# Half of the first product's column groups as two Strassen units, pooling moved into the second product, batch 2 pooled as rows

## The chip, the cores and the metric

The kernel runs on one core of one Trainium2 chip. The metric is the device time in microseconds (us) of the slowest core, here the only one. Profile pages are of one execution. "Fast" and "slow" are the two states of a run: slow is a run more than 1.5% above the fastest of the same kernel, and verdicts use fast runs only. "Faster" and "slower" ask for a ratio clear of 2%; within that is "same". Engines are called PE (the matrix engine), DVE (vector), ACT (scalar), POOL and SP; the last two issue transfers here.

## The reference, cut to what matters

```python
# q, k, v: (8 batches, 8 heads, 576, 64); w_in: (512, 2048); w_out: (2048, 512)
k_p = k.reshape(B, H, 72, 8, D).mean(axis=3)        # keys and values pooled by 8
v_p = v.reshape(B, H, 72, 8, D).mean(axis=3)
attn = softmax(q @ k_p^T / 8)
x = (attn @ v_p) -> (4608 tokens, 512)
h = x @ w_in                                         # first product, "up"
out = silu(h) @ w_out                                # second product, "down"
```

## The kernel before

Tokens go through in nine tiles of 512. Tile t has an up (16 groups of 128 columns of `w_in`, four matmuls of 512 columns each) and a down. From tile 1 on, the down is one Strassen level: seven products of quarters in place of eight, with sums of weights made once (`weight_sum`) and sums of the hidden values made in each tile (`hidden_sum`). Beside tile t's down PE computes the attention of batch t+1, which gives `xT` for the next tile. One core's engines work through their own queues in program order, and the program places small work ("fillers") between matmuls by step numbers.

```python
def spread(fillers, n):                 # a filler at step i is put behind step i
    todo = sorted(fillers, key=lambda f: f[0])
    for i in range(n):
        yield i
        while todo and todo[0][0] <= i:
            todo.pop(0)[1]()
...
def select_v(b, a, tag="at"):           # pooled rows -> heads, by selection matmuls
    if a == 0:
        st["v_ps"] = ps_tile([128, H, D], FP32, tag, "v_ps")     # one bank for both halves
    ... nc.tensor.matmul(st["v_ps"][:SP, h, :], lhsT=shifts[...], rhs=v5[:n, i], ...)
def copy_v(b, a, copy=nc.vector.tensor_copy):
    copy(out=vp[:, heads of half a], in_=v_ps[:SP, heads of half a])
...
def numerators(b, g, f):                # 8 matmuls, then two multiplies on DVE:
    nc.vector.tensor_mul(out=xT[:, 2 * g + c, cols], in0=nu[c][:, :HS], in1=rec)
...
# down_quarters: product order and the first sums on DVE
KA = KQ - 2
product(2, 0, KA); product(5, 0, KA); product(2, KA, KQ)
nc.vector.tensor_copy(out=r_sb, in_=ps["P"])
product(5, KA, KQ)
tt(out=rr_sb, in0=ps["Q"], in1=r_sb, op=add)
...
# schedule of tile t, a = t + 1 (cut)
items = [(g, 0, NTT) for g in range(KG)]                  # 16 plain groups
f_up.append((0, lambda: pool_k(a)))                       # pooling beside the up
f_up.append((10, lambda: pool_v(a)))
f_up.append((1, lambda: load_one(a + 1, "k")))            # first half of the next keys (SP)
f_up.append((2, lambda: load_rest(a + 1, "k")))           # second half, added by the transfer (POOL)
f_down: scores at steps 1, 28, 56, 77; denominators 28, 46, 69, 89; numerators 46, 69, 89, 93
```

The softmax here doesn't subtract the row's maximum and nothing guards it: scores larger than these inputs give would overflow.

## Time and profile before

| | before |
|---|---|
| time, median of the runs beside the changed kernel | 295.86 us (295.78 to 296.62) |
| span in the profile | 294.7 us |
| PE busy / idle | 287.9 / 6.8 us |
| DVE, ACT busy | 65%, 60% |
| start of tile 1; tiles 1 to 8 (us each) | 54.2; 31.7 30.6 30.1 30.5 30.3 30.8 26.0 30.5 |

A tile's length is read from PE's timeline, from its first matmul to that of the next tile. Two more rows of the page matter: the busy tenths of PE in 40 equal slices of the span, and the clock that PE was granted in them.

```profile
PE   8999999999999999999999999999999999999995
...
PEclk9999999999999999999999999999999999999998
```

In every slice between the first and the last PE is busy for 90% or more, and its granted clock is 90% or more. In the lines below, names in `_ps` are buffers in PSUM that matmuls write: `hp_ps` and `u_ps` for the up, `o_ps` for the down, `sc_ps`, `den_ps` and `nu_ps` for scores, denominators and numerators, `kz_ps` and `v_ps` for selected keys and values; `xT` is the input of the up, `h_T` the hidden values, `es` the exponentials.

### The profile page before, as it was taken

How to read it: one execution, taken by the hardware profiler on the slowest of the kernel's cores; microseconds unless marked ns; L12 is line 12 of the kernel's file. 1: busy time of each engine (PE TensorE's matmuls, PEld its weight loads, DVE VectorE, ACT ScalarE, POOL GpSimd, SP SyncE). 2: the span in 40 equal slices, each digit the busy share in tenths (PEclk: the TensorE clock that was granted, in tenths of full speed). 3: DMA queues.
4: the chain of work that ended last, by engine and by line, in shares of the span. 5: the costliest groups of instructions: out<-in, count | busy, mean ns of one | idle time of the engine just before them, and what ended most of it. 6: DMA issues, size and time to landing. Idle time of an engine off the chain costs nothing.

```text
span 294.7 us, 6052 instructions
## 1 busy us (share of the span) xinstructions
PE 287.9 (98%) x2417; PEld 175.6 (60%) x2417; DVE 191.2 (65%) x344; ACT 177.6 (60%) x366; POOL 42.8 (15%) x60
## 2 busy tenths in 40 slices
PE   8999999999999999999999999999999999999995
PEld 3348434446564666457788774476547654884584
DVE  4886445999978566865586659666865642741562
ACT  1677675567566865676667675776577666407500
POOL 8654100001300120013001710110000000000000
PEclk9999999999999999999999999999999999999998
DMA  7999999958794797487857895783500032004003
GB/s 215 271 282 205 247 229 180 209 147 174 106 177 108 160 132 136 106 177 111 150 128 162 120 122 137 167 116 51 123 20 2 2 89 53 2 22 117 6 12 135
DMA packets 34909, 37.65 MB, mean 128 GB/s; under 512 B 9856, under 2 KB 26368, under 8 KB 34880
## 3 DMA queue, kind: packets, MB, share of 16 engines
q0 software_dynamic: 20128, 18.50, 37.3%
q1 hardware_dynamic: 14176, 17.84, 26.5%
q10 hardware_dynamic: 576, 0.92, 0.9%
q8 instruction: 19, 0.31, 0.5%
q14 instruction: 10, 0.08, 0.1%
HBM read 36.70 MB, written 9.44 MB: 157 GB/s over the span
## 4 chain that ended last, share of the span: by engine, by line
PE 86%; DVE 10%; ACT 1%; issue 1%; DVEq 0%
PE hp_ps L428 37%; PE o_psQ L535 14%; PE o_psP L535 14%; PE o_psR L535 4%; PE sc_ps L348 4%; PE o_ps L462 4%; PE warm_ps L583 4%; PE nu_ps L388 3%; DVE raw L197 3%; DVE h_sum L495 2%; PE den_ps L365 2%; DVE w_sum L513 2%; DVE qT L148 1%; DVE xT L396 1%; PE kz_ps L313 1%
## 5 line engine op out<-in xcount | busy, mean ns | idle before, releaser
L428 PE MATMUL hp_ps<-xT,w_in_sb 128*128 128x512 bf16 (+3 forms) x684 | 128.2, 345 | 0.4 <-ACT h_T L434 0.4
L434 ACT ACTIVATE h_T<-hp_ps 128x512 bf16<-128x512 f32 (+2 forms) x155 | 87.4, 567 | 57.4 <-PE hp_ps L428 45.3
L428 PEld LDWEIGHTS <-w_in_sb 128*128 128x128 bf16 x684 | 65.9, 98 | 56.6 <-issue 1.5
L495 DVE TENSOR_TENSOR h_sum<-h_T 128x1024 bf16<-128x1024 bf16 (+2 forms) x88 | 52.0, 637 | 36.1 <-ACT h_T L434 36.1
L535 PEld LDWEIGHTS <-h_sum 128*128 128x128 bf16 x640 | 60.9, 98 | 15.1 <-issue 6.5
L356 ACT ACTIVATE es<-sc_ps 72x288 bf16<-72x288 f32 x128 | 41.4, 403 | 13.2 <-PE sc_ps L348 13.1
L396 DVE TENSOR_TENSOR xT<-nu_ps,rec 128x288 bf16<-128x288 f32 x64 | 25.7, 448 | 12.0 <-PE nu_ps L388 11.8
L535 PEld LDWEIGHTS <-h_T 128*128 128x128 bf16 x256 | 23.6, 98 | 6.5 <-issue 4.1
L177 POOL DMA_DIRECT2D raw<-in_k_dram x5 | 7.1, 1420 | 114.5 <-DVE h_sum L495 48.4
L148 DVE STREAM_TRANSPOSE qT<-q_bf 128x576 bf16<-128x576 bf16 x32 | 23.6, 758 | 0.0
L374 ACT ACTIVATE lnd<-den_ps 128x288 f32<-128x288 f32 x30 | 12.3, 411 | 16.6 <-PE nu_ps L388 9.8
L197 DVE TENSOR_TENSOR raw<-raw 72x1024 f32<-72x1024 f32 (+1 forms) x18 | 19.7, 1094 | 0.1
L291 DVE TENSOR_TENSOR raw<-raw 128x768 f32<-128x768 f32 (+3 forms) x16 | 10.5, 654 | 11.1 <-DMA raw<-in_v_dram 7.8
L535 PE MATMUL o_psP<-w_out_sb,h_sum 128*128 128x256 bf16 x128 | 17.6, 273 | 0.0
L535 PE MATMUL o_psQ<-w_out_sb,h_sum 128*128 128x256 bf16 x128 | 17.6, 273 | 0.0
L535 PE MATMUL o_psQ<-w_sum,h_T 128*128 128x256 bf16 x128 | 17.5, 274 | 0.0
L535 PE MATMUL o_psP<-w_sum,h_sum 128*128 128x256 bf16 x128 | 17.0, 273 | 0.5 <-DVE o_sb L556 0.5
L535 PE MATMUL o_psP<-w_sum,h_T 128*128 128x256 bf16 x128 | 16.5, 273 | 0.0
L535 PE MATMUL o_psR<-w_sum,h_sum 128*128 128x256 bf16 x128 | 16.5, 273 | 0.0
L462 PE MATMUL o_ps<-w_out_sb,h_T 128*128 128x512 bf16 x64 | 15.9, 381 | 0.0
L535 PE MATMUL o_psQ<-w_sum,h_sum 128*128 128x256 bf16 x128 | 15.4, 273 | 0.0
L348 PE MATMUL sc_ps<-qT,kz 32*72 32x288 bf16 x256 | 14.4, 295 | 0.9 <-DVE xT L396 0.7
(58 smaller groups left out, 212.0 us busy)
## 6 DMA issues: line engine op xcount, KB each, us to landing
out_dram<-o_sb SPq DMA_DIRECT2D x128, 64.0 KB, 1.7
raw<-in_k_dram SPq DMA_DIRECT2D x8, 512.0 KB, 5.2
raw<-in_v_dram SPq DMA_DIRECT2D x7, 512.0 KB, 6.9
q_bf<-in_q_dram POOLq DMA_DIRECT2D x6, 576.0 KB, 11.8
raw<-in_k_dram POOLq DMA_DIRECT2D x5, 576.0 KB, 9.1
raw<-in_v_dram POOLq DMA_DIRECT2D x5, 576.0 KB, 9.9
w_in_sb<-in_moe_w_in_dram POOLq DMA_DIRECT2D x8, 256.0 KB, 8.5
w_out_sb<-in_moe_w_out_dram POOLq DMA_DIRECT2D x4, 512.0 KB, 13.7
```

The costliest lines, as they stand in the source:

```text
L148: nc.vector.transpose(out=st["qT"][:, a, f * QF : (f + 1) * QF].rearrange("r i c p -> r (i c p)"), in_=st["q_bf"][:, a, f * n : (f + 1) * n],)
L197: nc.vector.tensor_add(out=raw[:, :, :w], in0=raw[:, :, :w], in1=raw[:, :, w : 2 * w])
L348: nc.tensor.matmul(sc[s], lhsT=kz[b % 2][rows, g, c, :], rhs=st["qT"][rows, g, f * QF : (f + 1) * QF, c, :], start=(c == 0), stop=(c == 1),)
L356: nc.scalar.activation(es[:, s, :], sc[s], func=AF.Exp, scale=score_scale)
L374: nc.scalar.activation(lnd, den_ps[:, :HS], func=AF.Ln)
L396: nc.vector.tensor_mul(out=xT[:, 2 * g + c, cols], in0=nu[c][:, :HS], in1=rec)
L428: nc.tensor.matmul(hp_ps[:, r0:r1], lhsT=w_in_sb[:, kk, g * 128 : (g + 1) * 128], rhs=xT[:, kk, x0 : x0 + r1 - r0], start=(kk == 0), stop= ...
L434: nc.scalar.activation(h_T[:, g, n0 : n0 + n], hp_ps[:, :n], func=AF.Silu)
L462: nc.tensor.matmul(ps, lhsT=h_T[:, g, m * 128 : (m + 1) * 128], rhs=w_out_sb[:, g, :], start=(g == 0), stop=(g == KG - 1),)
L495: nc.vector.tensor_tensor(out=h_sum[n][:, ks, :], in0=quarter(*a, ks), in1=quarter(*b, ks), op=op)
L535: nc.tensor.matmul(ps[b][:, c, :], lhsT=left(n, kt, c), rhs=W_OUT[n][:, kt, :], start=b not in begun, stop=kt == KQ - 1, skip_group_check= ...
L583: nc.tensor.matmul(warm_ps, lhsT=warm[:, :128], rhs=warm, start=True, stop=True)
```

## The change

The intent is fewer matmuls. Column groups 4 to 7 and 8 to 11 of the up become Strassen "units" (the first of them only in tile 1, both in tiles 2 to 8): seven products of four matmuls of 256 columns, 28 in place of 16 of 512. Sums of `w_in` are made once in tile 0, five sums of `xT` in every tile, four sums from PSUM per unit, all on DVE. To make room, pooling of the keys goes into the down of the tile before, pooling of the values and two of four q transposes go into the down of the same tile, and two copies go to ACT. Batch 2, which was loaded as heads, is loaded as pooled rows and selected by matmuls; that frees buffer space. Products 2 and 5 of the down now begin with their second halves (KA is KQ // 2), whose column groups are ready first. Cut to its core:

```diff
+    def stage(y, n):                       # unit y, product n
+        if n == "2": product(y, 2, "P", True);  nc.scalar.copy(r_sb, ps["P"])
+        elif n == "5": product(y, 5, "Q", True);  tt(out=rr_sb, in0=ps["Q"], in1=r_sb, op=ALU.add)
+        elif n == "1": product(y, 1, "R", True);  tt(out=t_sb, in0=ps["R"], in1=rr_sb, op=ALU.subtract)
+        elif n == "4": product(y, 4, "P", False); hidden(y, 1, 0, ps["P"])      # Silu
+        elif n == "3": product(y, 3, "Q", False); hidden(y, 0, 1, ps["Q"])
+        elif n == "7": product(y, 7, "P", False); tt(out=c_sb[0], in0=ps["P"], in1=t_sb, op=ALU.add)
+        ...
...
-            items = [(g, 0, NTT) for g in range(KG)]
+                items = (G(12, 13) + [(0, "251")] + G(14) + [(0, "43")] + G(15) + [(0, "76")]
+                    + [(1, "2")] + [(0, "s")] + [(1, "51")] + G(0) + [(1, "43")] + G(1)
+                    + [(1, "76")] + G(2) + [(1, "s")] + G(3))
+            for n in U_X:
+                f_up.append((0, lambda n=n: unit_x_sum(t, n)))
+            for n in (2, 5, 1, 6):
+                f_up.append((46 if t == 1 else 36, lambda n=n: hidden_sum(n, 4, 8)))
+            for n in (2, 5, 1):
+                f_up.append((64, lambda n=n: hidden_sum(n, 0, 4)))
+            f_down.append((60, lambda: hidden_sum(6, 0, 4)))
...
+            elif t == 1:                    # batch 2 as rows
+                    f_down.append((8 + 10 * j, lambda j=j: slot_sums("v", j)))
+                    f_down.append((40 + j, lambda j=j: select_v(2, j, "at")))
+                    f_down.append((40 + j, lambda j=j: copy_v(2, j)))
             else:
-                f_up.append((0, lambda: pool_k(a)))
+                f_down.append((10, lambda: pool_v(a)))
...
+                for y in range(2):          # tile 0
+                    for n in U_W:
+                        f_up.append((22 + 14 * y, lambda y=y, n=n: unit_weight_sum(y, n)))
+                    f_down.append((43 + 7 * j, lambda j=j: slot_sums("k", j)))
             elif a + 1 < B:
+                f_down.append((50, lambda: pool_k(a + 1, 0)))
+                f_down.append((81, lambda: pool_k(a + 1, 1)))
                 f_up.append((1, lambda: load_one(a + 1, "k")))     # kept where it was
                 f_up.append((2, lambda: load_rest(a + 1, "k")))
```

## The prediction

> **What bounds the kernel now.** I read the page's busy shares first, then the chain that ended last in order of time, then the timelines of VectorE (DVE) and ScalarE (ACT) around the places where that chain leaves TensorE (PE). The page and the per-core view give clock 0.997 and:
>
> ```profile
> PE 287.9 (98%) x2417; PEld 175.6 (60%) x2417; DVE 191.2 (65%) x344; ACT 177.6 (60%) x366; POOL 42.8 (15%) x60
> ```
>
> PE is idle for only 6.8 us of 294.7. The kernel has nine token tiles (t = 0 to 8), each with a first product ("up") and a second ("down"). The chain prices both:
>
> ```profile
> 238.30 13.81 PE hp_ps L428 x64
> ...
> 257.35 1.75 PE o_psP L535 x16
> ```
>
> A plain up of 64 matmuls of 512 columns takes 13.81 us, 0.2158 each; 16 matmuls of 256 columns take 1.75 us, 0.109 each, although each has its own weight load of 98 ns: the load hides. The windows by tile give 30.1 to 30.8 us for tiles 2 to 6, 26.0 for tile 7 (no attention beside it), 30.4 for tile 8 with its tail. So work removed from PE is worth its full time, as long as nobody makes PE wait.
>
> The 65% of DVE hides one place where DVE is already the bound. From 50.3 to 77.4 us the chain runs on DVE; its timeline is gapless at the end of tile 0:
>
> ```profile
> 48.35 0.82 DVE L396 TENSOR_TENSOR xT<-nu_ps,rec 128x288 bf16<-128x288 f32 x2 [0.45 <-PE nu_ps L388]
> 49.35 0.69 DVE L470 COPY o_sb<-o_ps 128x512 f32<-128x512 f32 x1 [0.18 <-PE o_ps L462]
> 49.95 0.81 DVE L396 TENSOR_TENSOR xT<-nu_ps,rec 128x288 bf16<-128x288 f32 x2
> 50.68 1.42 DVE L513 TENSOR_TENSOR w_sum<-w_out_sb 128x512 bf16<-128x512 bf16 x4
> 52.02 0.81 DVE L396 TENSOR_TENSOR xT<-nu_ps,rec 128x288 bf16<-128x288 f32 x2
> 52.75 1.42 DVE L513 TENSOR_TENSOR w_sum<-w_out_sb 128x512 bf16<-128x512 bf16 x4
> 54.09 0.81 DVE L396 TENSOR_TENSOR xT<-nu_ps,rec 128x288 bf16<-128x288 f32 x2
> ```
>
> The last pair writes the xT that tile 1's first group reads in its third and fourth matmul; PE starts that group at 54.37, so it comes some 0.3 us early, no more. The end of that DVE chain is the only real wait of PE in mid-kernel:
>
> ```profile
> 77.39 0.40 PE L348 MATMUL sc_ps<-qT,kz 32*72 32x288 bf16 x5 [0.67 <-DVE xT L396]
> ```
>
> Three of eight score matmuls ran, the fourth wanted a PSUM buffer that DVE had yet to empty: five buffers rotate, and the third scores of a tile reuse the first numerators' buffer.
>
> A steady tile has slack instead. Tile 3 (up ends, "T0", at 130.5):
>
> ```profile
> 131.18 1.28 ACT L401 ACT_TABLE_LOAD   x1
> 132.47 1.30 ACT L356 ACTIVATE es<-sc_ps 72x288 bf16<-72x288 f32 x4
> ```
> ```profile
> 131.19 1.36 DVE L495 TENSOR_TENSOR h_sum<-h_T 128x512 bf16<-128x512 bf16 x3 [0.89 <-ACT h_T L434]
> 134.10 0.69 DVE L548 COPY r_sb<-o_psP 128x512 f32<-128x512 f32 x1 [1.54 <-PE o_psP L535]
> 134.71 1.22 DVE L495 TENSOR_TENSOR h_sum<-h_T 128x2048 bf16<-128x2048 bf16 x1
> 135.84 0.68 DVE L550 TENSOR_TENSOR rr_sb<-o_psQ,r_sb 128x512 f32<-128x512 f32 x1
> 137.34 0.82 DVE L396 TENSOR_TENSOR xT<-nu_ps,rec 128x288 bf16<-128x288 f32 x2 [0.82 <-PE nu_ps L388]
> ```
>
> Before the first numerators are emptied DVE idles 1.54 + 0.82 us, and the third scores come at 138.5, another 0.8 after the first buffer is free. The exponentials end at 133.77 and the denominators want them at 134.1.
>
> **What the Trainium skill says.** "TensorE: Matmul & The Clock Gate", Wait — 56ns, not 53.3ns?: start to start is N/2.4 + about 2.5 ns warm, 109 ns for N = 256; the trace agrees (1.75/16). "VectorE: DVE Perf Modes", The perf-mode tier table: tensor_tensor is 2x in bf16 from SBUF and 1x with a PSUM operand; the trace has 0.355 us a step for 512 bf16 elements (1.42 for four) and 0.61 (0.69 alone) for 512 with a PSUM operand. "PSUM — Partial Sum Buffer", Engine vs sequencer instructions: the queues of VectorE and ScalarE are strict FIFO; the timelines agree, each keeps the program's order, so a sum placed ahead of a numerator delays it in full.
>
> **The change, part by part.**
>
> *PE.* A unit replaces four groups, 16 x 0.2158 = 3.45 us, by 28 matmuls of 256 columns, 28 x 0.109 = 3.06: 0.39 saved. One unit in tile 1, two in tiles 2 to 8: 15 units, -5.9 us. Batch 2 as rows brings 24 + 12 selection matmuls (12 moved PE by 0.2 to 0.3 us in tile 0, 6 by 0.2 to 0.3) less four transposes (0.13): about +0.8. Net -5.1 us: this alone would give 290.7.
>
> *DVE, steady tile.* Added: five x sums (5 x 0.355 = 1.8) and four PSUM sums a unit (8 x 0.61 = 4.9). Removed: key copy 0.3 and one output copy 0.61, both to ACT. Net +5.8 on 20 to 21 us a tile, some 26.5 of 29.5: near 90%. Moved from up into down: pooling, two q transposes, one hidden sum: 4.65 + 1.4 + 0.6 us. The down side goes from about 9.6 to 15.7 us against 16.2 of PE.
>
> *DVE, tile 0.* Ten w_in sums (3.55 us) go ahead of batch 1's key row sums; batch 2's key row sums (1.86 + 1.43) and the first piece of w_sum 4 (0.36) go ahead of the last numerators. Tile 1 loses two head trees of pooling (each two trees of about 2.3 us) and gets value row sums (3.3), copies (1.4), its unit and x sums (4.3) and pooling for batch 3 (2.0): no lighter.
>
> Now the places in order.
>
> (a) Tile 0, key selection: the row sums end at 25.4 and 26.9, PE wants them at 28.2 and 29.3; pushed by 3.55 they end at 29.0 and 30.4. PE waits about 1.1 us.
>
> (b) Start of tile 1: 1.86 + 1.43 + 0.36 = 3.65 us more in a gapless DVE queue with 0.3 of slack: 3.3 us of PE wait.
>
> (c) First numerators of tile 1: they need the values' copy, which stands behind the last w_sum pieces 1.1, x sums 1.8, unit 2.5, copies 0.6, transposes 1.4, w_sum 7 and half of 6 2.1, hidden sums 2.4 + 1.8, transpose 0.7, value row sums 3.3, r_sb 0.6, hidden sum 7 1.1, transpose 0.7, rr 0.6, copy 0.4: 21 us from the end of (b), plus about 2 in which DVE waits for PE. PE gets there 2.9 us sooner; before lost 0.67 nearby: +2.2.
>
> (d) Tiles 2 to 6. In up, unit 1's last PSUM sums stand behind four hidden sums (4 x 0.6), which wait for t_sb, about 9.4 us into the up: DVE reaches them at 11.8 instead of 11.0, and the ACT queue ends its last Silu about 1.65 us after T0 instead of 0.7. Table load and exponentials then end at T0 + 4.2, where the denominators want them at 3.7: half a microsecond of wait. From that last Silu DVE has, before the first numerators are emptied: hidden sums 1.8, transpose 0.7, value pooling 1.85, r_sb 0.61, hidden sum 7 1.13, transpose 0.7, rr 0.61, first multiply 0.37 = 7.8: T0 + 9.4, against scores at T0 + 8.0. Both waits together: 1.35 us in tiles 2 and 3. Tiles 4 to 6 empty four numerators there, and scores need the third: T0 + 10.2 against 8.2, 1.9 us. Sum 2 x 1.35 + 3 x 1.9 = 8.4. Were ACT not late at all (0.7), it would still be 2 x 0.3 + 3 x 0.8 = 3.0. I take the middle, 5.7.
>
> (e) Tiles 7 and 8: the second part of product 2 comes 1.75 us after T0, its hidden sum at 2.3: 0.5; tile 8 hides most of it in the 0.52 us that its product 7 waited before: 0.15.
>
> Sum: -5.1 + 1.1 + 3.3 + 2.2 + 5.7 + 0.6 = +7.8: 303.6 us. I say 303.5.
>
> **The rivals.**
>
> *The gain arrives.* PE is 98% busy, DVE and ACT are at 65 and 60%, so the added sums fill idle time and 290 to 292 remain. For it: the shares, and a matmul schedule that leaves 1 to 2 us for every sum inside the units. Against it: the idle time of DVE is in up and at fixed points, the additions in (b) and (d) stand in a FIFO ahead of what PE wants next. For (b) I see no way round.
>
> *DVE becomes the bound throughout.* Then the tile lasts 26.5 us of DVE work plus its waits for PE and ACT, some 3.6 us (1.8 in the units, 1.65 at T0): about 30.1 to 31.5, and with (a) to (c) 305 to 308.
>
> *Transfers.* Batch 2's keys arrive on POOL's queue behind w_out, which landed at 43.4; 1.2 MB behind it at the 0.29 MB/us of that stretch is there by 47.5, before DVE asks at 49. Pooling for the next batch is now asked for about 23.5 us into a tile, while its second half is issued about 15 us in and takes 9.1 (page, issues): it could cost up to 1 us a tile, 3 in all: 306.
>
> **Range and chances.** The low end has (d) at 3.0, (c) at 1 and (a) hidden: 298.6; with a unit chain looser than I drew it, 297.5. The high end has (d) at 8.4 and late keys: 308. The 2% line is at 301.8. (b) plus the low (d) already eats the 5.1 us, so faster by over 2% is very unlikely; whether it stays under 301.8 hangs on (c) and (d).
>
> **What would show it.** Matmul cost: units at 0.109 us a matmul and up of tiles 7 and 8 near 13.0 us. (a): PE idle at about 28 us with DVE's key row sums as releaser. (b): 3 us of PE wait on xT at the start of tile 1. (c): numerators of tile 1 waiting for the vp copy. (d): in tiles 2 to 6 denominators waiting for es and the third scores waiting for xT, 1 to 2 us a tile, DVE near 90%. I am wrong if PE stays 98% busy and tiles 2 to 6 last 29.6 us; then the time is 291 to 293. If only (b) and (c) show, it is about 298.

## More of the kernel before

The stores of a tile's results stand in SP's queue at the end of its down, ahead of the loads of the next keys.

The waits of PE between 15 and 100 us (what waited, for whom, us in all, how often, the longest) are three, and small:

```profile
PE sc_ps L348 <- DVE xT L396: 0.7, 1, 0.7
PE hp_ps L428 <- ACT h_T L434: 0.4, 1, 0.4
PE sc_ps L348 <- DVE qT L148: 0.3, 1, 0.3
```

## The result, and the profile after

| | before | after |
|---|---|---|
| median of four fast runs | 295.86 us | 318.80 us (316.40 to 319.72) |
| span in the profile | 294.7 | 314.6 |
| start of tile 1 | 54.2 | 56.5 |
| tiles 1 to 8 | 31.7 30.6 30.1 30.5 30.3 30.8 26.0 30.5 | 39.6 31.3 31.6 35.6 31.6 32.0 26.1 30.4 |

The ratio is 1.0764, with a 95% interval of 1.0708 to 1.0821: slower. A ratio here is the mean time of one kernel's fast runs over that of the other's in the same rounds, so not quite the ratio of the medians; a fifth fast run (319.56 us) counts in it. The profile is of the fastest of the runs, 316.4 us; the others have no trace. In the two traces 19.9 us were added, and the tiles place them: tiles 0 and 1 together +10.2 (before ended them at 85.9, after at 96.1), tiles 2 to 6 +9.8, of which tile 4 alone +5.1, tiles 7 and 8 together -0.1.

The page of the changed kernel, its busy shares and the same two rows:

```profile
PE 293.3 (93%) x2597; PEld 192.3 (61%) x2597; DVE 235.2 (75%) x429; ACT 184.4 (59%) x393; POOL 46.2 (15%) x62
...
PE   8998999699599999999899969999999999999985
...
PEclk9999999999899999999999997999999999999999
```

PE is idle for 21.3 us now. More than that: it is busy for 5.4 us longer although less was asked of it, and in or just behind two of the three gaps of PE's row (the 5 and the second 6) the clock row shows a drop. The page's chain that ended last accounts for only some 5% of this span and can't be used; the list of PE's waits from 15 us on can:

```profile
PE sc_ps L323 <- DVE xT L371: 4.6, 7, 2.1
PE v_ps L306 <- DVE vp L313: 3.9, 1, 3.9
PE hp_ps L510 <- DVE xT L371: 2.8, 2, 1.5
PE o_psP L615 <- DVE h_sum L575: 2.5, 7, 0.7
PE kz_ps L288 <- DVE kz L295: 0.9, 2, 0.5
PE kz_ps L288 <- DVE k L270: 0.6, 1, 0.6
```

The third line, and of the last two the 0.61 and 0.45 us that fall in tile 0 (the keys of batch 1), are about as the prediction drew them. The rest comes in the places below.

**Start of tile 1.** DVE's timeline at the end of tile 0 has the new key row sums (L266) and the piece of `w_sum` ahead of the last numerators:

```profile
49.73 1.54 DVE L266 TENSOR_TENSOR raw<-raw 128x768 f32<-128x768 f32 x2
...
53.91 1.14 DVE L266 TENSOR_TENSOR raw<-raw 128x512 f32<-128x512 f32 x2
...
58.04 0.81 DVE L371 TENSOR_TENSOR xT<-nu_ps,rec 128x288 bf16<-128x288 f32 x2
```

The last pair starts at 58.04, 3.95 us later than it did (54.09). PE waits twice here, 1.45 us for the last pair but one and 1.33 us for the last (the first two lines of the next view).

**The values of batch 2, in tile 1's down.** PE's timeline:

```profile
56.47 0.74 PE L510 MATMUL hp_ps<-xT,w_in_sb 128*128 128x512 bf16 x2 [1.45 <-DVE xT L371]
58.54 3.33 PE L510 MATMUL hp_ps<-xT,w_in_sb 128*128 128x512 bf16 x14 [1.33 <-DVE xT L371]
...
79.01 0.27 PE L615 MATMUL o_psR<-w_sum,h_sum 128*128 128x256 bf16 x1
83.14 0.48 PE L306 MATMUL v_ps<-v,shifts 128*72 128x64 bf16 x6 [3.86 <-DVE vp L313]
```

The first half of the values was selected at 78.81; the second half goes into the same PSUM tile, whose first copy DVE reached only at 82.69. What came then is in the windows view (start and end, us; busy time of PE, PEld, DVE, ACT, POOL with counts; granted clock; share and rate of transfers), cut where the granted clock changes:

```profile
79.28:83.14 3.86, 0.00 (x1) 0.00 (x0) 3.78 (x7) 0.11 (x1) 0.00 (x0) 1.00 0.63 153
...
83.66:87.07 3.41, 3.41 (x24) 1.49 (x24) 2.03 (x5) 0.86 (x2) 2.17 (x2) 0.50 0.02 2
87.07:90.48 3.41, 3.41 (x43) 2.32 (x42) 2.72 (x6) 2.32 (x7) 0.00 (x0) 1.00 0.90 123
```

PE went on at 83.14, still at full clock; from 83.66 to 87.07 it was granted half, and then all of it again. That stretch lost 3.41 x 0.50 = 1.7 us, on top of the 3.86 of the wait, and the wait list doesn't show it.

**Keys of the next batch, tile 4.** Key pooling now stands at step 50 of the down, ahead of numerators. In tile 4 the keys were not there. SP's queue in that stretch (start, us, transfers issued):

```profile
158.12 11.83 SPq L530 DMA_DIRECT2D out_dram<-o_sb  x16
170.05 1.17 SPq L172 DMA_DIRECT2D raw<-in_k_dram  x2
```

POOL's timeline, with the second half's issue:

```profile
176.17 1.41 POOL L181 DMA_DIRECT2D raw<-in_k_dram  x1 [18.29 <-DVE h_sum L575]
```

DVE's timeline, where it pools the keys:

```profile
186.05 1.22 DVE L187 TENSOR_TENSOR raw<-raw 72x1024 f32<-72x1024 f32 x1 [2.59 <-DMA raw<-in_k_dram]
```

And PE's:

```profile
188.30 0.40 PE L323 MATMUL sc_ps<-qT,kz 32*72 32x288 bf16 x5 [2.12 <-DVE xT L371]
```

The tile began at 158.95. SP was busy issuing the 16 stores of the tile before and came to the keys' first half 11 us into the tile; POOL issued the second half, which is added onto the first, at 17; it was usable at 27. DVE waited 2.59 us, the numerators behind it came late, PE waited 2.12 us for a PSUM buffer, and its clock dropped again:

```profile
186.06:189.47 3.41, 1.29 (x16) 0.88 (x13) 2.96 (x5) 0.82 (x3) 1.13 (x2) 1.00 0.08 16
189.47:192.89 3.42, 3.42 (x26) 1.86 (x25) 1.78 (x6) 2.22 (x5) 3.42 (x7) 0.50 0.65 78
192.89:196.30 3.41, 3.41 (x25) 2.30 (x24) 2.27 (x5) 1.00 (x2) 1.52 (x3) 1.00 1.49 149
```

That is 3.42 x 0.50 = 1.7 us once more.

**Every tile from 2 to 6, behind T0 (the end of the up).** Tile 2, T0 at 109.4, DVE's timeline:

```profile
111.09 1.89 DVE L575 TENSOR_TENSOR h_sum<-h_T 128x1024 bf16<-128x1024 bf16 x3 [1.59 <-ACT h_T L516]
112.91 0.77 DVE L152 STREAM_TRANSPOSE qT<-q_bf 128x576 bf16<-128x576 bf16 x1
113.60 1.18 DVE L187 TENSOR_TENSOR raw<-raw 72x1024 f32<-72x1024 f32 x1
114.82 0.69 DVE L192 TENSOR_TENSOR vp<-raw 72x512 bf16<-72x512 f32 x1
115.43 0.68 DVE L628 COPY r_sb<-o_psP 128x512 f32<-128x512 f32 x1
116.03 1.21 DVE L575 TENSOR_TENSOR h_sum<-h_T 128x2048 bf16<-128x2048 bf16 x1
...
118.43 0.80 DVE L371 TENSOR_TENSOR xT<-nu_ps,rec 128x288 bf16<-128x288 f32 x2
```

After 1.59 us of idling for ACT's last Silu there is no gap until the first numerators are emptied at T0 + 9.0. PE pays at three points: it waits 0.22 us for the hidden sum, its four denominator matmuls take 0.64 us where later ones of the same tile take 0.31 (they wait for the exponentials inside the group), and it waits 0.54 us for the scores' buffer.

```profile
111.84 1.05 PE L615 MATMUL o_psP<-w_out_sb,h_sum 128*128 128x256 bf16 x8 [0.22 <-DVE h_sum L575]
...
113.37 0.64 PE L340 MATMUL den_ps<-es,ones 72*32 72x288 bf16 x4
...
118.92 0.40 PE L323 MATMUL sc_ps<-qT,kz 32*72 32x288 bf16 x5 [0.54 <-DVE xT L371]
```

### The profile page after: what moved, and what is told of

It reads as the page before. It is cut to its first block, busy times and chain, and to the rows that moved or that the text cites. A ratio compares the mean times of both kernels' runs of the same rounds, so it can differ in the third digit from the quotient of the medians.

```text
span 314.6 us, 6608 instructions
## 1 busy us (share of the span) xinstructions
PE 293.3 (93%) x2597; PEld 192.3 (61%) x2597; DVE 235.2 (75%) x429; ACT 184.4 (59%) x393; POOL 46.2 (15%) x62
## 5 line engine op out<-in xcount | busy, mean ns | idle before, releaser
L510 PE MATMUL hp_ps<-xT,w_in_sb 128*128 128x512 bf16 (+3 forms) x412 | 82.7, 340 | 3.2 <-DVE xT L371 2.8
L516 ACT ACTIVATE h_T<-hp_ps 128x512 bf16<-128x512 f32 (+2 forms) x95 | 51.6, 546 | 38.3 <-PE hp_ps L510 37.5
L575 DVE TENSOR_TENSOR h_sum<-h_T 128x1024 bf16<-128x1024 bf16 (+1 forms) x72 | 50.2, 743 | 12.9 <-ACT h_T L516 11.8
L510 PEld LDWEIGHTS <-w_in_sb 128*128 128x128 bf16 x412 | 39.2, 98 | 28.4 <-issue 3.2
L452 PEld LDWEIGHTS <-w_sum 128*128 128x128 bf16 x300 | 29.4, 98 | 7.7
L460 ACT ACTIVATE h_T<-c_sb 128x512 bf16<-128x512 f32 x30 | 18.9, 629 | 16.0 <-DVE c_sb L484 16.0
L266 DVE TENSOR_TENSOR raw<-raw 128x768 f32<-128x768 f32 (+3 forms) x24 | 15.6, 651 | 9.9 <-DMA raw<-in_v_dram 6.4
L323 PE MATMUL sc_ps<-qT,kz 32*72 32x288 bf16 x256 | 17.7, 295 | 5.3 <-DVE xT L371 4.6
L615 PE MATMUL o_psP<-w_sum,h_sum 128*128 128x256 bf16 x128 | 18.1, 285 | 0.2 <-DVE o_sb L637 0.2
L472 DVE TENSOR_TENSOR rr_sb<-u_psQ,r_sb 128x512 f32<-128x512 f32 x15 | 10.4, 692 | 8.8 <-ACT r_sb L469 8.8
```

The lines of the kernel that those rows point to most:

```text
L266: nc.vector.tensor_add(out=raw[..., :w], in0=raw[..., :w], in1=raw[..., w : 2 * w])
L323: nc.tensor.matmul(sc[s], lhsT=kz[b % 2][rows, g, c, :], rhs=st["qT"][rows, g, f * QF : (f + 1) * QF, c, :], start=(c == 0), stop=(c == 1),)
L452: nc.tensor.matmul(ps[bank][:, u, :], lhsT=w[:, kk, 128 * u : 128 * (u + 1)], rhs=x[:, kk, :], start=first and u == 0 and kk == 0, stop=kk ...
L460: nc.scalar.activation(h_T[:, g : g + 2, j * NQ : (j + 1) * NQ], src, func=AF.Silu)
L510: nc.tensor.matmul(hp_ps[:, r0:r1], lhsT=w_in_sb[:, kk, g * 128 : (g + 1) * 128], rhs=xT[:, kk, x0 : x0 + r1 - r0], start=(kk == 0), stop= ...
L516: nc.scalar.activation(h_T[:, g, n0 : n0 + n], hp_ps[:, :n], func=AF.Silu)
```

## The experiments

The theory after reading the traces: the added work fits, its places in the queues don't. Four places cost the time: late keys, the end of tile 0, the values' copy in tile 1, and the chain behind T0. The rivals: the units themselves are what costs (then a kernel without them returns to the time before), and DVE is simply too full (then no order of the same work helps). All edits are against the changed kernel. In each group of rounds the kernel before was timed on the same chip: 296.21 us for runs 1 to 4, 296.45 for 5 to 8, 296.36 for 9 and 10 (medians). At 2%, runs 1 to 5 are slower than the kernel before and runs 6 to 10 the same.

**1. No units.** All 16 groups plain, no sums of `w_in` or `xT`, all else as changed.

```diff
-            items = (... units ...)
+            items = G(12, 13, 14, 15, 4, 5, 6, 7, 8, 9, 10, 11, 0, 1, 2, 3)
-            unit_x_sum(t, n) ...      # and tile 0's unit_weight_sum(y, n)
```

> The changed kernel with all 16 column groups plain in every tile: no units, no x sums, no w_in sums; the rest of the change (batch 2 as rows, pooling and transposes moved into the second product, copies on ACT) stays. Theory (order in DVE's queue and late keys, not the units alone): PE has 5.9 us more matmul, but tile 0's key selection no longer waits (-1.1), tile 1 loses 4.3 us of DVE work before the values' copy (-4 to -5), ACT is not late at the start of the second product, so the waits of tiles 2 to 6 fall from about 9 to 3 or 4 us (-5 to -6): 311 to 313, still some 5% above the kernel before. Rival (the units are the cost, the rest is neutral): 295 to 298.

Measured: median 320.70 us of four runs, two of them (the profiled one too) slow; the two fast ones gave 319.66 and 316.58, ratio 1.0741 (1.0679 to 1.0802). The rival "the units cost the time" falls: without them the kernel is no faster. The number that I expected is missed too. The profile fell in the slow state, so no difference of times is taken from it; its waits are listed as they stand. PE's:

```profile
PE sc_ps L323 <- DVE xT L371: 8.3, 5, 4.8
PE v_ps L306 <- DVE vp L313: 3.9, 1, 3.9
```

DVE's for a key transfer:

```profile
DVE raw L187 <- DMA raw<-in_k_dram: 9.2, 3, 5.3
```

They suggest why nothing was gained: a DVE with less to do asks for the late keys sooner and stands longer in front of them, and the values' wait is as before. That is read from one slow run; the next ones test it.

**2. Keys earlier.** The keys for the tile after next are loaded as soon as their buffer has been pooled, ahead of the stores of that tile.

```diff
-                f_up.append((1, lambda: load_one(a + 1, "k")))
-                f_up.append((2, lambda: load_rest(a + 1, "k")))
+                if t == 1: ...                       # as it was
+                if a + 2 < B:
+                    f_down.append((82, lambda: load_one(a + 2, "k")))
+                    f_down.append((83, lambda: load_rest(a + 2, "k")))
```

> The changed kernel, but the key loads of the batch after next are issued at step 82 of the second product, ahead of the output stores in the DMA queue, as soon as the buffer is free; nothing else moves. Theory: DVE's waits for raw<-in_k_dram (0.94 us in tile 3, 2.59 in tile 4 of the profile, perhaps more in the slower timed runs) vanish, and with them the clock loss behind the 2.12 us wait of PE in tile 4: tile 4 falls from 35.6 to about 31.6 us, the whole to 312 to 315. Rival (the waits for keys are only in front of a DVE that is late anyway): within 1 us of 318.8.

Measured: 313.57 us (311.54 to 313.74), ratio 1.0571 (1.0538 to 1.0605), as expected: 5.2 us less by the medians. Tile 4 lasts 31.6 in place of 35.6 us, tile 3 30.8 in place of 31.6, and no key wait of DVE is left there. Late keys cost some 5 us. In the two traces the whole gains only 2.7 us (314.6 to 311.9): tiles 3 and 4 gain 4.7, but tile 1 loses 2.3, because the clock is halved there for longer (59.11 to 62.52 and 83.0 to 89.8, in place of 83.66 to 87.07). The two waits at its start, 1.46 and 1.33 us, are as they were; here half clock follows them, in the changed kernel's profile it did not (its clock was 1.00 from 52.94 to 63.18).

```profile
55.70:59.11 3.41, 1.29 (x4) 0.40 (x5) 3.41 (x11) 1.26 (x1) 0.00 (x0) 1.00 0.54 135
59.11:62.52 3.41, 3.41 (x9) 1.22 (x8) 2.44 (x8) 1.19 (x2) 0.00 (x0) 0.50 0.59 154
```

**3. Tiles 0 and 1 lighter.** The ten sums of `w_in` go to tile 0's down, batch 2's key row sums behind the last numerators, `w_sum` 4 into tile 1's up, and tile 1 has no unit.

```diff
-                        f_up.append((22 + 14 * y, lambda y=y, n=n: unit_weight_sum(y, n)))
+                        f_down.append((2, lambda y=y, n=n: unit_weight_sum(y, n)))
-                    f_down.append((43 + 7 * j, lambda j=j: slot_sums("k", j)))
+                    f_down.append((58, lambda j=j: slot_sums("k", j)))
-            (4, 0, f_down, 57, (0, PW)),
+            (4, 1, f_up, 30, (0, PW)),
```

> The changed kernel with tiles 0 and 1 put in another order: the ten w_in sums in the second product of tile 0, where DVE idles; batch 2's key row sums behind tile 0's last numerators; w_sum 4 in tile 1; no unit in tile 1. Theory: the 10.2 us that tiles 0 and 1 lost against before come from what stood in front of the numerators in DVE's queue, so 8 to 10 us come back: 309 to 311. Rival (DVE has too much to do in these tiles whatever the order; the unit left out takes only 4 us off it): 314 to 316.

Measured: 314.10 us (312.35 to 316.60), ratio 1.0623 (1.0558 to 1.0689): 4.7 us less, short of what I expected. PE's waits on `xT` at the start of tile 1 and its waits on the keys' row sums are gone, but the values' wait is 3.9 us still, and tile 4's wait for late keys grew from 2.1 to 3.8. So the queue in front of the values' copy is made in tile 1's own down, not carried over from tile 0.

**4. Runs 2 and 3 together.** Both edits.

> Both edits together. Theory: they are different waits in different tiles, so they add: 303 to 306, with 5 us of waits left in tiles 2 to 6 (0.2 for the hidden sum, 0.3 for denominators, 0.5 to 0.6 for the third scores in each). Rival (one hides the other): above 308.

Measured: 307.98 us (306.77 to 308.31), ratio 1.0391 (1.0368 to 1.0414), above what I expected. The gains add up (10.8 against 5.2 + 4.7), but the values' wait is untouched:

```profile
79.02 0.65 PE L306 MATMUL v_ps<-v,shifts 128*72 128x64 bf16 x6 [3.86 <-DVE vp L313]
```

**5. Values' row sums in the up.** Run 4, and batch 2's value row sums go from tile 1's down into the end of its up.

```diff
-                    f_down.append((8 + 10 * j, lambda j=j: slot_sums("v", j)))
+                    f_up.append((56 + j, lambda j=j: slot_sums("v", j)))
```

> Early keys and the new order of tiles 0 and 1, and batch 2's value row sums (3.2 us of DVE) moved from the second product of tile 1 to the end of its first, where DVE idles 2.9 us for ACT. Same work on every engine. Theory: the second value selection of tile 1 waits 3.86 us because DVE's queue from the last Silu to the values' copy is 8.9 us long; 3.2 us shorter, PE waits about 1 us, its clock does not fall, and tile 1 goes from 38.8 to 33 us: 301.5 to 303. Rival (DVE has too much work in tile 1, so the wait only moves): 306 to 308.

Measured: 302.93 us (302.31 to 303.01), ratio 1.0217 (1.0201 to 1.0232), as expected. The same six matmuls now wait 0.91 us, the clock is 1.00 throughout tile 1, and tile 1 lasts 33.5 in place of 38.8 us: 5.3 us less, of which the wait is 3.86 - 0.91 = 2.95. The rest, 2.3 us, fits what the clock cost run 4: in its trace PE was granted half clock from 77.77 to 84.60 and was busy from 79.02 on, 5.58 us, which is at most 2.8 us lost.

```profile
75.54 0.48 PE L306 MATMUL v_ps<-v,shifts 128*72 128x64 bf16 x6 [0.91 <-DVE vp L313]
```

**6. The chain behind T0 shorter.** Run 4, and value pooling goes back into the up, while the second-half hidden sums move from step 36 to 52 so that they no longer stand ahead of unit 1's sums.

```diff
-                f_up.append((46 if t == 1 else 36, lambda n=n: hidden_sum(n, 4, 8)))
+                f_up.append((46 if t == 1 else 52, lambda n=n: hidden_sum(n, 4, 8)))
-                f_down.append((10, lambda: pool_v(a)))
+                f_up.append((36, lambda: pool_v(a)))
```

> Early keys and the new order of tiles 0 and 1, and in tiles 2 to 8 two moves of DVE work, nothing added or taken: the pooling of the values goes to step 36 of the first product, the four hidden sums from step 36 to 52, behind unit 1's last PSUM sums. Theory (order): ACT is on time at the start of the second product, the queue before the first numerators is 1.85 us shorter, and tiles 2 to 6 lose nearly all of their waits (9 us in all): about 29.3 to 30.0 us each, 299 to 301. Rival (DVE at 26 us of work a tile is the bound, whatever the order): tiles 2 to 6 stay at 31 to 32 us, 307 to 309.

Measured: 301.63 us (300.71 to 301.71), ratio 1.0170 (1.0154 to 1.0186), slightly above what I expected. Tiles 2 to 6 last 1.0 to 1.5 us less each (30.3 29.9 30.1 30.1 30.6), still more than they could: waits for hidden sums remain.

**7. Runs 5 and 6 together.**

> All four edits: early keys, tiles 0 and 1, values up, lighter second product. Theory: the savings add, 292.5 to 295, just below the kernel before. Rival (throughput): 301 or more.

Measured: 295.99 us (295.61 to 296.22), ratio 0.9985 (0.9968 to 1.0002): level with the kernel before, a microsecond more than I expected. PE still waits for hidden sums early in each down: 0.16 to 0.20 us at its first matmul in tiles 2 to 6, 0.49 at the other half of product 2 in tiles 7 and 8:

```profile
PE o_psP L615 <- DVE h_sum L575: 1.9, 7, 0.5
```

**8. Run 7 without units.** The schedule of run 7 with the items of run 1.

> The kernel with all four edits, but every column group plain: no units, no x sums, no w_in sums. Where nothing waits for DVE, the 14 units (two in tiles 2 to 8) are worth 14 x 0.39 = 5.5 us of PE, so this one should be 4 to 5.5 us slower than with units: 297.5 to 300. Rival (a unit gives back on DVE and ACT what it saves on PE): as fast as the kernel with units or faster.

Measured: 297.47 us (297.37 to 297.50), ratio 1.0036 (1.0021 to 1.0051), just under the range. Tiles 2 to 7 are those of the kernel before to 0.01 us (30.56 30.08 30.49 30.33 30.80 26.04), so the moved pooling costs nothing once it is well placed; batch 2 as rows, with what else tiles 0 and 1 do differently, makes these two end 1.5 us later (87.4 against 85.9), and tile 8 is 0.6 us shorter, so that this run is 1.0 us above the kernel before. Against run 7 the units were worth only 1.5 us, because run 7's tiles still waited.

**9. Fewer sums behind T0.** Run 7, and only the two hidden sums that the down needs first (2 and 5) stay early; sum 1 is made whole at the end of the up, sum 6 inside the down, value pooling at step 52.

```diff
-            for n in (2, 5, 1, 6):
+            for n in (2, 5):
                 f_up.append((46 if t == 1 else 36, lambda n=n: hidden_sum(n, 4, 8)))
-            for n in (2, 5, 1):
+            for n in (2, 5):
                 f_up.append((64, lambda n=n: hidden_sum(n, 0, 4)))
-            f_down.append((60, lambda: hidden_sum(6, 0, 4)))
+            f_up.append((64, lambda: hidden_sum(1, 0, 8)))
+            if a >= B: f_up.append((52, lambda: hidden_sum(6, 4, 8)))
+            f_down.append((60, lambda: hidden_sum(6, 0, 8 if a < B else 4)))
-                f_up.append((36, lambda: pool_v(a)))
+                f_up.append((52, lambda: pool_v(a)))
```

> The kernel with all four edits still waits some 0.4 to 0.5 us a tile at the start of the second product for hidden sums 2 and 5, which now stand behind the value pooling and the units' last sums. Here hidden sums 2 and 5 of column groups 4 to 7 go back to step 36, the value pooling to step 52, and hidden sum 6 into the second product; same work. Theory: the queue then has what PE wants first in front, the waits go, tiles 2 to 6 take 29.4 to 30.0 us: 292 to 293.5 in all, 1% below the kernel before, and 4 to 5 us below the same edits without units (297.5), the units' full worth. Rival (DVE is simply full): 295.5 to 296.5.

Measured, with five rounds: 292.82 us (292.69 to 293.14), ratio 0.9888 (0.9871 to 0.9904), as expected: 1.1% less than the kernel before, with an interval clear of 1, though inside the 2%. The waits that the expectation put at 0.4 to 0.5 us a tile were 0.2 in tiles 2 to 6 of run 7; these tiles got 0.3 to 0.55 us shorter. The busy shares of its page:

```profile
PE 283.8 (98%) x2585; PEld 189.0 (65%) x2585; DVE 229.8 (79%) x406; ACT 184.0 (63%) x392; POOL 46.0 (16%) x62
```

The largest waits of PE behind its start:

```profile
PE v_ps L306 <- DVE vp L313: 1.2, 1, 1.2
PE o_psP L615 <- DVE o_sb L637: 0.6, 1, 0.6
```

PE waits for no hidden sum and no scores' buffer any more (what is left below these two is 0.4 us and less, apart from the 1.2 us of the start). In tile 2 the first numerators are emptied 7.5 us after the down's first matmul (107.96 less 100.44); in the changed kernel it was 9.2 (118.43 less 109.24). DVE has 229.8 us of work against 235.2 in the changed kernel, and is busier as a share: the rival "DVE is too full" falls with this run. Tile 3 lasts 29.30 us against 30.08 in run 8, tile 7 25.24 against 26.04: there two units are worth 0.8 us; in tiles 2, 4 and 5 it is 0.57 to 0.66.

**10. Two more copies on ACT.** Run 9, with the copy of batch 2's values and the last tile's copy of product 4 on ACT.

```diff
-                    f_down.append((40 + j, lambda j=j: copy_v(2, j)))
+                    f_down.append((40 + j, lambda j=j: copy_v(2, j, nc.scalar.copy)))
-            copy = nc.vector.tensor_copy if last else nc.scalar.copy
-            copy(o_sb[1][:, cs, LO], ps["P"][:, cs])
+            nc.scalar.copy(o_sb[1][:, cs, LO], ps["P"][:, cs])
```

> As the one before, with batch 2's two value copies and the last tile's copy of product 4 on ACT, which is idle there. Theory: the 0.92 us wait of the second value selection in tile 1 and the 0.2 us of product 7 in the last tile go: 1 us less, 291 to 292.5. Rival (ACT's own queue delays them as long): no difference.

Measured, with five rounds: 292.44 us (291.77 to 292.81), ratio 0.9869 (0.9851 to 0.9887), inside the expected range. But the interval overlaps that of run 9, so the two are not told apart, and the 1 us that the edit was to gain is not shown by the times (in the traces the wait for the values fell from 1.16 to 0.41 us and tile 1 from 33.75 to 33.01). Both intervals lie below 1.

## Why the prediction was right or wrong

The direction was right (slower by over 2%), the size was not: 303.5 us with 308 as the upper end, against 318.8. In the profiles 19.9 us were added where the sum said 7.8. Three steps failed: (c) let PE run past the place where it stopped and left out the clock, late keys stood outside the sum, and (d) was cut to the middle. By its steps:

- **PE: right, a little generous.** Two units save 0.78 to 0.80 us in tiles 3, 6 and 7 and 0.57 to 0.66 in tiles 2, 4 and 5 (run 8 against run 9); the sum had 2 x 0.39.
- **(a) and (b), keys of batch 1 and start of tile 1: right.** PE's waits for the keys of batch 1 in tile 0 are 0.61 + 0.45 = 1.06 us (1.1 was predicted), those on `xT` 1.45 + 1.33 = 2.8 (3.3). The 0.3 us of slack in (b) took PE's start for 54.37; the trace has 54.21, so about half of it was there, which changes the term little. Run 3, which takes both away and tile 1's unit with them, gains 4.7.
- **(c), "First numerators of tile 1 ... +2.2": mis-placed and too small.** The DVE queue that I added up was there, but I let PE run on to the numerators. It stopped seven steps sooner, at the second half of the values' selection, since both halves share one PSUM tile. The Trainium skill, "PSUM — Partial Sum Buffer", PSUM bank collisions raise a hardware error, has the rule that PSUM is to be guarded by bank and quadrant, not by address; the trace agrees as far as it goes, a write into other columns of the bank waited 3.86 us for a read. (Whether the program guards by bank or by buffer can't be told here, as the buffer is one bank.) Then the clock fell, which the sum had nowhere: 1.7 us. Run 5 takes 5.3 us out of tile 1 by moving the row sums alone. So the term was 2.2 and should have been about 5 (3.86 + 1.7 less the 0.67 that the kernel before lost nearby).
- **(d), "I take the middle, 5.7": the total of the working was right, the cut to the middle wrong.** The full chain, drawn from durations, said 1.35, 1.35, 1.9, 1.9, 1.9 us for tiles 2 to 6, 8.4 in all. Run 2, where keys are no longer late, against run 9, where these waits are gone, gives 31.30 - 29.96 = 1.34, then 1.54, 1.78, 1.81 and 2.03: 8.5. That it agrees so well is partly luck: in tile 2 the visible parts are 0.22 us for the hidden sum, which (d) did not have, 0.33 for the denominators, drawn as 0.5, and 0.54 for the scores. I had assumed that ACT might be less late than drawn; the last Silu came 1.7 us after T0, exactly as drawn (1.65).
- **Late keys, a rival of "up to 1 us a tile, 3 in all", left out of the sum: it came true and was larger.** Run 2 prices it at 5.2 us. I had seen when POOL issues the second half, but took its moment (15 us into the tile) from the kernel before; there the stores and key loads had ended in time for pooling beside the next up, and nobody waited. In tile 4 it was issued at 17 and landed at 27. The 2.12 us wait cost another 1.7 us of clock.
- **(e): right in kind, too small.** PE waits 0.7 us in each of tiles 7 and 8 for the hidden sum, where 0.5 and 0.15 were predicted (in tile 8 an older wait fell from 0.52 to 0.23), and that eats what the units saved there.
- **The rival "DVE becomes the bound throughout": wrong.** Runs 5, 6, 7 and 9 do nearly the same work (one unit of fifteen fewer) in another order and end 16 to 26 us sooner than the changed kernel. The work itself was priced right: DVE is busy for 25.2 to 26.2 us in each of tiles 2 to 6, where the sum had 26.5.

In the profiles the miss of 12.1 us is: tiles 0 and 1, 10.2 against 7.0 predicted (a 1.1, b 3.3, c 2.2, rows 0.8, less one unit 0.4), so 3.2; tiles 2 to 6, 9.8 against 1.8 predicted (5.7 less ten units, 3.9), so 8.0, of which tiles 3 and 4 in run 2 show 4.7 to be late keys, 2.8 is the cut to the middle (8.5 less 5.7), and 0.5 is that ten units save 3.4 us there (run 8 against run 9) and not 3.9; tiles 7 and 8, -0.1 against -0.9, so 0.8; rounding leaves 0.1. Beside that, the median is 2.4 us above the profiled run. What the other runs lost more than it is open: they have no trace, and with granted clocks of 0.988 and 0.989 against 0.989 it was not the clock in the runs of the median. The range was built a little too narrow as well: the high end's own terms, (d) at 8.4 and late keys at 3, add up to 309.4 and not 308.

## What to carry to other kernels

A share of busy time doesn't say whether added work fits: nearly the same sums cost 23 us or gave 3.5, depending on what they stood ahead of in a queue that runs in order. When work is moved to an earlier place, look at who must have delivered its input by then, and behind what that transfer was queued. When a chain drawn from durations says a wait is 8.4 us, don't halve it for comfort, and where PE would idle for some 2 us out of 3.4, add the clock that it costs afterwards.

## What the Trainium skill lacked or had wrong

- "TensorE: Matmul & The Clock Gate", Why this matters for your kernels, says to keep gaps between matmul bursts under about 3 us. Here a wait of 2.12 us (186.18 to 188.30) was followed by half clock from 189.47 to 192.89, a loss of 1.7 us, so the margin is smaller than the page says. What the traces show instead: in each of them the clock changes lie on a grid of 3.41 us (in the changed kernel 83.66 and 189.47 are 31 steps apart). In the step before each of the eleven drops in mid-kernel (runs 1 to 4 and 6, and the changed kernel) PE had idled for 2.01 to 3.41 us; no step in mid-kernel that began at full clock and had 1.67 us or less of idling brought one. So it is partly chance: the waits of 1.46 and 1.33 us at the start of tile 1 fell into one step in run 2 (2.12 us idle, a drop) and into two in the changed kernel's profile (1.34 and 1.44, no drop). Between 1.67 and 2.01 us no run shows anything. The two states of full and half clock and the step of 3.41 us agree with the page's Part 1, which lets the clock fall after an idle window of that length; the window need not be wholly idle.
- "DMA: Bandwidth & Descriptors", Issuing engines are not separate DMA queues, calls the time to initiate a transfer usually small relative to the transfer. For one transfer that holds here too (0.74 us a store on SP, its waits for earlier stores included, against a median of 1.7 us from issue to landing over the run). What the page doesn't say is that issues add up in a queue: SP took 11.83 us for 16 stores of 64 KB in a row, and the loads behind them were issued 11 us into the tile; putting the loads ahead was worth 5.2 us (run 2).
